# Issuing the clears of a scatter target before two batches' routing instead of behind it

## The chip, the cores and the metric

The kernel runs on one core of a Trainium2 chip. The metric is device microseconds (us) of one execution; the time of a kernel is the median over its runs. The profile is of one execution of its own.

## What is computed

An attention block, then two mixture-of-experts layers with top-1 routing, all in float32.

```python
# attention, per batch (4) and head (8): 512 tokens and 32 states of 64
a  = softmax(x @ state.T / 8);   xread = a @ state
a2 = softmax(state @ x.T / 8);   sread = a2 @ x
x  = concat(xread, sread)  ->  2176 rows of 512

# layer 1 (with a capacity per expert) and layer 2 (without), 8 experts
logits = x @ w_gate
e, gate = argmax(logits), softmax(logits)[argmax]
out[i]  = gate[i] * (relu(x[i] @ w1[e]) @ w2[e])     # w1: 512x1024, w2: 1024x512
# layer 1: a token beyond its expert's capacity gives a row of zeros
```

## The kernel before

**Rows in DRAM.** Attention writes its 2176 rows to `xrows`, 513 words each: 512 values and the gate. The values go out by batch, the gate column later by stores of single words, two per batch (L667, L668, inside `route`). Layer 1 gathers its tokens from `xrows` and scatters its results to `yrows`, of the same shape, from which layer 2 gathers. A token over capacity is never scattered, so `yrows` is first cleared as a whole: `fills` issues four DMAs from a tile of zeros (L711).

**Stages.** An expert's tokens are worked off in quads of 4 x 128 tokens, one quad to a stage. The first stage of a layer is that of the most popular expert, whose first tokens are listed early, before all batches are routed. A stage runs eight columns of `m1_quad` (h = relu(x w1), L1062 to L1065) and `m2_quad` (y += h w2, L1073), interleaved: `(1,0) (1,1) (2,0) (1,2) (2,1) ... (2,7)`. Float32 products are made from hi and lo parts. ScalarE casts the hi part and GpSimd or VectorE subtracts to get the lo part, for weights (`wsplit`, L277 and L278; `split1`, L1291 and L1292) and for tokens and h alike. Beside the quads, experts with few rows left run alone as "small" experts straight from the raw weights (L1221).

**The end of a stage.** `tail` runs the last columns of a stage. Among them it puts the gathers of the next quad's tokens on GpSimd (`gather`, L580), the casts of the next w1's first halves on ScalarE (`split1`, L1291), and the transposes of the gathered tokens on TensorE (`x_quad`, L1032). Each engine works in program order, so a cast that waits for its weights holds the ReLU (L1064) behind it.

**Queues.** Weights, row stores, clears and the zeroing of the output are all issued by SP, in program order, on one DMA queue. Gathers and scatters are GpSimd's own, on another. The next expert's weights (`wload`, L273) can be issued only when the chip has counted the tokens: `planned(0)` copies the counts to `ri` (L1507), and SP reads its branch and the expert's number from there. In the first stage four chunks of w1, four of w2 and eight for a small expert are issued in this order.

**The background list.** What is not TensorE's main work stands in a list of generators, `bgq`, and is woven into the program when it is built. `tick(n)` takes up to n steps of the generator at its head and goes on to the next when that one ends. The first layer's first stage calls `tick(4)` after each part of a column (three parts for `m1_quad`, four for `m2_quad`). A generator that yields `PAUSE` ends the tick; `abreast` takes steps of several in turn and pauses only when all of them do. When the stage begins, the rest of `route(1, 1)` (the second batch's routing) is still at the head. The list then gets the routing of the third and fourth batch (`route(2, 2)`, which ends with their gate stores) abreast of the second batch's list (`enlist_batch(1)`); the clears (`fills`, one step); the plan of the stages (`plan_runs`) abreast of the last two lists; and the reading out of the lists (`plan_lists`).

Of the kernel before, what the change touches and what calls it, by code (L numbers as in the profile page):

```python
# [74 lines left out]
def moe_kernel(ctx: ExitStack, tc: tile.TileContext, x, state, wg1, w1a, w2a, cap, wg2, w1b, w2b, out):  # L75
# [24 lines left out]
    bgq = deque()  # L100
# [14 lines left out]
    def named(name, g):  # L115
        yield from g
        done.add(name)
# [9 lines left out]
    def abreast(*gs):  # L127


        gs = [[g, -1] for g in gs]  # L130
        while gs:
            n = 0
            for s in list(gs):
                if s[1] == clock[0]:
                    continue
                n += 1
                try:
                    if next(s[0]) is PAUSE:
                        s[1] = clock[0]
                    else:  # L140
                        yield
                except StopIteration:
                    gs.remove(s)
            if not n:
                yield PAUSE
# [240 lines left out]
    def list_out(pool, L, g, m, sv, u, w):  # L386

        if g is not None:
            DVE.tensor_scalar(g, sv, -1.0, 0.0, op0=ALU.add, op1=ALU.max)
            yield  # L390
        DVE.tensor_scalar(u, sv, 0.5, FAR, op0=ALU.is_lt, op1=ALU.mult)
        DVE.tensor_scalar(m[:, :, 2], sv, 0.5, None, op0=ALU.is_gt)
        yield
        DVE.scalar_tensor_tensor(out=m[:, :, 3], in0=sv, scalar=-1.0, in1=u, op0=ALU.add, op1=ALU.add)
        yield
        if L == 0:
            DVE.tensor_scalar(w, m[:, :, 3], 1.0 / P, 0.5 / P - 0.5, op0=ALU.mult, op1=ALU.add)
            yield
            DVE.tensor_scalar(m[:, :, 0], w, MAGIC, MAGIC, op0=ALU.add, op1=ALU.subtract)
            yield  # L400
            DVE.scalar_tensor_tensor(out=w, in0=m[:, :, 0], scalar=-float(P), in1=m[:, :, 3], op0=ALU.mult, op1=ALU.add)
            yield
            DVE.tensor_scalar(m[:, :, 1], w, 1.0, None, op0=ALU.add)
            yield
# [141 lines left out]
    def plan_lists(pool, L):  # L546

        mk, no = rt.pop("plan")
        la = pool.tile([KH, 2, P], F32, tag="la", name="la")
        lb = pool.tile([KH, 2, P], F32, tag="lb", name="lb")  # L550
        DVE.tensor_copy(lb, listp[:, :, 1])
        yield
        DVE.scalar_tensor_tensor(out=la, in0=listp[:, :, 0], scalar=float(P), in1=lb, op0=ALU.mult, op1=ALU.add)
        yield PAUSE
        for h in range(2):
            PE.matmul(pyv[:, 0:NT], la[:, h], mk[:, h], start=(h == 0), stop=(h == 1))
        sel = pool.tile([P, NT], F32, tag="sel", name="sel")
        DVE.tensor_copy(sel, pyv[:, 0:NT])
        yield
        DVE.tensor_scalar(rows[L], sel, -1.0, 0.0, op0=ALU.add, op1=ALU.max)  # L560

        ss = sel[:, ML * QT:NT]
        DVE.tensor_scalar(no, no, ss[:, 2 * NA:2 * NA + 1], None, op0=ALU.mult)
        yield
        DVE.tensor_tensor(out=no, in0=no, in1=ss[:, 0:2 * NA].rearrange("p (a b) -> p a b", b=2)[:, :, 0], op=ALU.add)
        yield
        DVE.tensor_scalar(rows1[L], no, -1.0, 0.0, op0=ALU.add, op1=ALU.max)
        u = pool.tile([P, NT], F32, tag="plu", name="plu")
        w = pool.tile([P, NT], F32, tag="plw", name="plw")
        yield from list_out(pool, L, None, md[L], sel, u, w)  # L570
# [6 lines left out]
    rp = ctx.enter_context(tc.tile_pool(name="route", bufs=1))  # L577
# [19 lines left out]
    def pauses(n):  # L597
        for _ in range(n):
            yield PAUSE

    def idle(n):
        for _ in range(n):
            yield
# [23 lines left out]
    def route(b0, nb, then=(), quick=False):  # L627

        n, run = nb * (R + 1), runs_[0]
        lg = lgs[:, b0:b0 + nb].rearrange("p b r e -> p (b r) e")  # L630
        gt = gts[:, b0:b0 + nb].rearrange("p b r -> p (b r)")
        ohb = rtp.tile([P, nb, R + 1, E], BF16, tag="oh", name="oh")
        oh = ohb.rearrange("p b r e -> p (b r) e")
        mv = []
        yield from argmax_onehot(rtp, lg, n, smask[:, 0:nb].rearrange("p b r -> p (b r)"), oh, mv)
        m, v = mv
        cs = rtp.tile([P, nb, R, E], BF16, tag="cs", name="cs")
        rs = rtp.tile([P, nb, 2, E], BF16, tag="rs2", name="rs2")
        DVE.tensor_copy(rs[:, :, 1], ohb[:, :, R])
        DVE.tensor_copy(cs[:, :, 1], ohb[:, :, 0])  # L640
        yield
        for r in range(2, R):
            DVE.tensor_tensor(out=cs[:, :, r], in0=cs[:, :, r - 1], in1=ohb[:, :, r - 1], op=ALU.add)
            yield
        DVE.tensor_tensor(out=rs[:, :, 0], in0=cs[:, :, R - 1], in1=ohb[:, :, R - 1], op=ALU.add)
        yield
        yield from pauses(QUICK[0]) if quick else idle(IDLE[0])
        w = nb * 2 * E
        rsv = rs.rearrange("p b a e -> p (b a e)")
        PE.matmul(pyv[:, 0:w], upper, rsv, start=True, stop=True)  # L650
        PE.matmul(pyv[:, w:2 * w], ones, rsv, start=True, stop=True)
        prs = rtp.tile([P, 2, nb, 2, E], F32, tag="prs", name="prs")
        DVE.tensor_copy(prs.rearrange("p t b a e -> p (t b a e)"), pyv[:, 0:2 * w])
        yield
        preb = rtp.tile([P, nb, R + 1, E], F32, tag="pre", name="pre")
        pre = preb.rearrange("p b r e -> p (b r) e")
        for i in range(nb):
            for a, r in ((0, 0), (1, R)):
                DVE.tensor_tensor(out=preb[:, i, r], in0=run, in1=prs[:, 0, i, a], op=ALU.add)
                DVE.tensor_tensor(out=run, in0=run, in1=prs[:, 1, i, a], op=ALU.add)  # L660
                yield
        yield from then

        def gates():
            yield from gate_of(rtp, lg, m, n, gt)
            for b in range(b0, b0 + nb):
                SP.dma_start(out=xrows[b * ST:b * ST + S, DM:ROW].rearrange("(p r) o -> p r o", p=P), in_=gts[:, b, 0:R, None])  # L667
                SP.dma_start(out=xrows[b * ST + S:(b + 1) * ST, DM:ROW], in_=gts[0:NS, b, R:R + 1])  # L668

        res = []  # L670

        def places():
            DVE.tensor_tensor(out=preb[:, :, 1:R], in0=cs[:, :, 1:R], in1=bc(preb[:, :, 0:1], [P, nb, R - 1, E]), op=ALU.add)
            yield
            far = rtp.tile([P, n, E], F32, tag="far", name="far")
            DVE.tensor_tensor(out=far, in0=pre, in1=bc(cape[:, None, :], [P, n, E]), op=ALU.is_ge)
            yield
            DVE.scalar_tensor_tensor(out=pre, in0=far, scalar=FAR, in1=pre, op0=ALU.mult, op1=ALU.add)
            yield
            yield from slots(rtp, oh, v, pre, n, res)  # L680

        yield from abreast(places(), gates())
        for i in range(nb):
            pp_[b0 + i] = [t[:, i * (R + 1):(i + 1) * (R + 1)] for t in res]
# [3 lines left out]
    def enlist_batch(b, quick=False, eng=(DVE, DVE, POOL)):  # L688

        pp, ek = pp_[b]  # L690
        todo = []
        for r in range(R + 1):
            np_ = P if r < R else NS
            oc = lsp.tile([P, NK], BF16, tag="loc", name="loc")
            ov = lsp.tile([P, 2, P], BF16, tag="lov", name="lov")
            yield from enlist(oc, ov, eng, np_, pp[:, r:r + 1], ek[:, r:r + 1], tida[:, b, r:r + 1], tidb[:, b, r:r + 1], todo)
            if len(todo) > LAG[b]:
                enlist_mm(*todo.pop(0))
        yield from pauses(QUICK[1]) if quick else idle(IDLE[1])
        while todo:  # L700
            enlist_mm(*todo.pop(0))
            yield from () if quick else idle(IDLE[2])
# [3 lines left out]
    def fills(*parts):  # L706

        g = NTOK // P
        for i in parts:
            lo, hi = g * i // 4, g * (i + 1) // 4  # L710
            SP.dma_start(out=yrows.rearrange("(g p) w -> p g w", p=P)[:, lo:hi], in_=bc(zeros[:, None, :], [P, hi - lo, ROW]))  # L711
        yield
# [813 lines left out]
    POOL.memset(meta, 0.0)  # L1526
    POOL.memset(ysb[:, 0], 0.0)
    POOL.memset(ysb[:, NY - 2:NY], 0.0)
    bgq += [abreast(route(2, 2, (), True), enlist_batch(1, True)), fills(0, 1, 2, 3), abreast(plan_runs(rp, 0), named("lists", chain(enlist_batch(2, True), enlist_batch(3, True)))), plan_lists(rp, 0)]
    for t in range(QT):  # L1530
        x_quad(t, ysb[:, 1 + t], py[t], gq[0])
    st = stage(0, 0, [(PLANNED[0], lambda: planned(0)), (READY, room)], TQ)
# [53 lines left out]
```

## Time and profile before

| | |
|---|---|
| median of 3 runs | 507.88 us (507.73 to 507.91) |
| profiled execution, own time | 511.39 us |
| its span, first to last instruction | 509.5 us |
| mean granted TensorE clock | 0.948 |
| TensorE (PE) matmuls, busy | 445.8 us (87%) |
| VectorE (DVE) busy | 195.2 us (38%) |
| ScalarE (ACT) busy | 165.9 us (33%) |
| GpSimd (POOL) busy | 216.5 us (42%) |
| SP's DMA queue: bytes, share of the 16 engines' span | 72.43 MB, 44.5% |
| GpSimd's DMA queue | 15.76 MB, 9.0% |

The shares are means over stages that differ. What holds TensorE in one stage is read from that stretch alone: the waits of TensorE and of the engine in front of it, and the DMA share of the stretch. A clock of 1.00 is 2.4 GHz, 0.50 is 1.2 GHz; a number between is a mean over a stretch that had both.

### The profile page before, as it was taken

What the parts mean: (1) busy time and instruction counts of PE and PEld (TensorE: products, weight loads), DVE (VectorE), ACT (ScalarE), POOL (GpSimd) and SP (SyncE); (2) the same over time, 40 slices, a digit from 0 to 9 for tenths busy, and PEclk for the clock granted to TensorE, in tenths of its full rate; (3) what the DMA queues carried; (4) which work ended last, traced back from release to release, by engine and by line L of the source; (5) the groups of instructions that cost most, each with busy time, mean ns of one, the idle gap of its engine ahead of it and who ended that gap; (6) DMA issues with size and microseconds to landing.
All of it is one profiled execution on the core that took longest, in us unless ns stands there. A gap on an engine that the chain in (4) does not pass through costs nothing. (4 is left out here: it accounts for less than half of the span.)

```text
span 509.5 us, 7964 instructions
## 1 busy us (share of the span) xinstructions
PE 445.8 (87%) x2629; PEld 326.0 (64%) x2629; DVE 195.2 (38%) x666; ACT 165.9 (33%) x288; POOL 216.5 (42%) x197
## 2 busy tenths in 40 slices
PE   8969586979879989999997959999999999999940
PEld 5647365757664775676874748778745847668830
DVE  7967757895040161041264041584410100411110
ACT  4647434210143412345311334312431213451010
POOL 6432742564413445415446403357553506774030
PEclk9999878988979999999999988999999999999995
DMA  8264757079989996909633100025997848200020
GB/s 244 72 151 117 206 135 202 1 175 182 316 305 364 371 381 196 366 24 346 251 132 122 43 11 4 0 95 193 376 388 267 318 171 279 94 28 1 3 93 3
DMA packets 47364, 89.49 MB, mean 176 GB/s; under 512 B 8592, under 2 KB 21136, under 8 KB 47248
## 3 DMA queue, kind: packets, MB, share of 16 engines
q1 hardware_dynamic: 42128, 72.43, 44.5%
q0 software_dynamic: 5120, 15.76, 9.0%
q8 instruction: 43, 0.70, 0.6%
q14 instruction: 73, 0.60, 0.4%
HBM read 67.70 MB, written 21.52 MB: 175 GB/s over the span
## 5 line engine op out<-in xcount | busy, mean ns | idle before, releaser
L1065 DVE SCALAR_TENSOR_TENSOR hTl<-ph,hTh 128x512 fp32r<-128x512 f32 x48 | 33.2, 691 | 206.3 <-ACT hTh L1064 194.8
L1073 PE MATMUL py<-w1h,hTh 128*128 128x512 f32 x192 | 82.6, 430 | 0.0
L1073 PE MATMUL py<-w1l,hTh 128*128 128x512 f32 x192 | 76.4, 398 | 0.0
L1073 PE MATMUL py<-w1h,hTl 128*128 128x512 f32 x192 | 76.4, 398 | 0.0
L278 POOL TENSOR_TENSOR w1l<-raw,w1h 128x1024 fp32r<-128x1024 f32 x22 | 52.6, 2395 | 53.3 <-ACT w1h L277 53.2
L1292 POOL TENSOR_TENSOR w0l<-raw,w0h 128x512 fp32r<-128x512 f32 x40 | 51.0, 1287 | 56.0 <-ACT w0h L1291 51.2
L1064 ACT ACTIVATE hTh<-ph 128x512 fp32r<-128x512 f32 x48 | 28.7, 597 | 127.3 <-PE ph L1062 89.2
L1062 PE MATMUL ph<-xTh,w0h 128*128 128x512 f32 x192 | 54.4, 406 | 7.4 <-issue 5.5
L1062 PE MATMUL ph<-xTl,w0h 128*128 128x512 f32 x192 | 57.2, 421 | 0.0
L1062 PE MATMUL ph<-xTh,w0l 128*128 128x512 f32 x192 | 55.5, 411 | 0.3 <-issue 0.3
L1062 PEld LDWEIGHTS ph<-xTh,w0h 128*128 128x128 f32 x192 | 36.3, 193 | 16.4 <-issue 8.8
L1062 PEld LDWEIGHTS ph<-xTl,w0h 128*128 128x128 f32 x192 | 36.0, 194 | 13.4 <-issue 6.6
L1073 PEld LDWEIGHTS py<-w1h,hTh 128*128 128x128 f32 x192 | 37.1, 193 | 9.5 <-issue 3.4
L1073 PEld LDWEIGHTS py<-w1h,hTl 128*128 128x128 f32 x192 | 36.9, 192 | 8.3
L1073 PEld LDWEIGHTS py<-w1l,hTh 128*128 128x128 f32 x192 | 37.2, 194 | 7.0 <-issue 1.0
L1062 PEld LDWEIGHTS ph<-xTh,w0l 128*128 128x128 f32 x192 | 35.3, 192 | 9.9 <-issue 3.4
L1091 POOL DMA_INDIRECT out_dram<-ysb,dsti x15 | 14.9, 993 | 60.2 <-ACT ysb L1081 52.1
L1291 ACT CAST w0h<-raw 128x512 fp32r<-128x512 f32 x40 | 24.0, 618 | 22.1 <-DMA raw<-in_moe_w_dram 20.8
L1091 POOL DMA_INDIRECT yrows<-ysb,dsti x16 | 15.9, 996 | 29.6 <-DVE oc L336 8.4
L277 ACT CAST w1h<-raw 128x1024 fp32r<-128x1024 f32 x24 | 25.1, 1045 | 5.9 <-issue 5.9
L340 POOL TENSOR_SCALAR lov<-iofb,rpp,tidb 128x128 bf16<-128x128 bf16 (+1 forms) x20 | 16.6, 838 | 15.0 <-DVE rek L330 15.0
L880 PE MATMUL pav<-vg,e1T 128*128 128x264 f32 x56 | 18.0, 450 | 1.2 <-ACT xr L881 1.2
(325 smaller groups left out, 646.5 us busy)
## 6 DMA issues: line engine op xcount, KB each, us to landing
raw<-in_moe_w_dram SPq DMA_DIRECT2D x104, 512.0 KB
out_dram<-zb SPq DMA_DIRECT2D x2, 2176.0 KB
xrows<-xr SPq DMA_DIRECT2D x16, 256.0 KB
yrows<-zeros SPq DMA_DIRECT2D x3, 1026.0 KB
xb<-in_x_dram SPq DMA_DIRECT2D x6, 512.0 KB
yrows<-zeros SPq DMA_DIRECT2D x1, 1282.5 KB
xb<-in_x_dram SPq DMA_DIRECT2D x4, 256.0 KB
st<-in_state_dram SPq DMA_DIRECT2D x1, 256.0 KB
```

The source lines that it names most:

```text
L277: ACT.copy(h, t)
L278: (POOL if on[c] else DVE).tensor_tensor(out=l, in0=t, in1=h.bitcast(F32), op=ALU.subtract)
L340: eng[2].tensor_scalar(ov[0:np_, 1], iofb[0:np_], pp[0:np_], tb[0:np_], op0=ALU.is_equal, op1=ALU.mult)
L880: PE.matmul(pv[:, a, 0:GW], e1_[b][:, r % 2, a, r // 2], vg[:, b, a], start=True, stop=True)
L1062: PE.matmul(p, w[k][:, 0, c * P:(c + 1) * P], u[:, k], start=(i == 0 and k == 0), stop=(i == 2 and k == NC1 - 1))
L1064: ACT.activation(out=hTh[:, c % 2], in_=p, func=AF.Relu)
L1065: DVE.scalar_tensor_tensor(out=hTl[:, c % 2], in0=p, scalar=0.0, in1=hTh[:, c % 2].bitcast(F32), op0=ALU.max, op1=ALU.subtract)
L1073: PE.matmul(py[t], u[:, c % 2, t * P:(t + 1) * P], w[c // 2][:, c % 2], start=(c == 0 and i == 0), stop=(c == NC2 - 1 and i == 2))
L1091: i = POOL.indirect_dma_start(out=(yrows if L == 0 else out)[:, :], out_offset=bass.IndirectOffsetOnAxis(ap=dsti[:, y:y + 1], axis=0), in_ ...
L1291: ACT.copy(h, t)
L1292: (POOL if ON[half][c] else DVE).tensor_tensor(out=l, in0=t, in1=h.bitcast(F32), op=ALU.subtract)
```

## The change

The clears move from the second place of the list to the first. They are then issued by SP in front of the third and fourth batch's gate stores instead of behind them.

```diff
-    bgq += [abreast(route(2, 2, (), True), enlist_batch(1, True)), fills(0, 1, 2, 3), abreast(plan_runs(rp, 0), named("lists", chain(enlist_batch(2, True), enlist_batch(3, True)))), plan_lists(rp, 0)]
+    bgq += [fills(0, 1, 2, 3), abreast(route(2, 2, (), True), enlist_batch(1, True)), abreast(plan_runs(rp, 0), named("lists", chain(enlist_batch(2, True), enlist_batch(3, True)))), plan_lists(rp, 0)]
```

## Rows read from the trace of the kernel before

**Rows 1.** Table of stretches: start:end, length, busy per engine, TensorE clock, DMA share, GB/s.
```profile
90.00:106.00 16.00, 15.78 (x76) 12.60 (x75) 13.49 (x58) 4.87 (x7) 8.17 (x9) 1.00 0.04 1
106.00:116.00 10.00, 6.42 (x26) 4.38 (x25) 9.70 (x50) 0.20 (x1) 6.82 (x8) 0.80 1.04 251
116.00:124.00 8.00, 8.00 (x36) 6.15 (x35) 3.23 (x11) 0.40 (x1) 1.72 (x3) 0.82 1.09 187
...
132.00:144.00 12.00, 7.60 (x37) 5.50 (x36) 1.72 (x3) 4.43 (x8) 5.12 (x4) 0.95 0.91 329
144.00:150.00 6.00, 6.00 (x20) 4.92 (x20) 3.00 (x10) 1.87 (x3) 0.00 (x0) 0.54 0.79 284
```

**Rows 2.** Timeline of SP's DMA queue: start, duration, issuing line.
```profile
86.99 0.61 SPq L668 DMA_DIRECT2D xrows<-gts  x1
102.90 0.52 SPq L667 DMA_DIRECT2D xrows<-gts  x1
...
105.47 3.46 SPq L711 DMA_DIRECT2D yrows<-zeros  x4
115.78 34.19 SPq L273 DMA_DIRECT2D raw<-in_moe_w_dram  x16
```

**Rows 3.** DMA issues of the page: size of one, count.
```profile
yrows<-zeros SPq DMA_DIRECT2D x3, 1026.0 KB
...
yrows<-zeros SPq DMA_DIRECT2D x1, 1282.5 KB
```

**Rows 4.** Timeline of ScalarE, first layer, first and fourth of four casts.
```profile
133.36 0.62 ACT L1291 CAST w0h<-raw 128x512 fp32r<-128x512 f32 x1 [7.99 <-DMA raw<-in_moe_w_dram]
...
141.83 0.62 ACT L1291 CAST w0h<-raw 128x512 fp32r<-128x512 f32 x1 [1.89 <-DMA raw<-in_moe_w_dram]
```

**Rows 5.** Timeline of TensorE, end of the first stage and start of the next.
```profile
135.77 0.39 PE L1073 MATMUL py<-w1h,hTh 128*128 128x512 f32 x1
...
138.05 0.66 PE L1032 MATMUL ph<-ident,xg 128*128 128x128 f32 x4 [1.44 <-DMA xg<-xrows,rows]
...
143.72 1.11 PE L1032 MATMUL ph<-ident,xg 128*128 128x128 f32 x4 [2.85 <-DVE hTl L1065]
...
150.82 1.08 PE L1062 MATMUL ph<-xTh,w0h 128*128 128x512 f32 x4
...
153.20 1.08 PE L1221 MATMUL pyT<-raw,xTf 128*64 128x512 f32 x4
```

**Rows 6.** Timeline of TensorE, the same instructions at a later stage's end.
```profile
217.64 0.39 PE L1073 MATMUL py<-w1h,hTh 128*128 128x512 f32 x1
...
221.73 0.60 PE L1032 MATMUL pyT<-ident,xg 128*128 128x128 f32 x4
...
224.94 1.09 PE L1062 MATMUL ph<-xTh,w0h 128*128 128x512 f32 x4
```

**Rows 7.** Timeline of GpSimd: gathers of the first stage, first, second and last.
```profile
125.05 1.10 POOL L580 DMA_INDIRECT xs<-xrows,rows  x1 [7.33 <-DVE md L392]
126.45 1.00 POOL L580 DMA_INDIRECT xg<-xrows,rows  x1 [0.30 <-issue]
...
130.36 1.00 POOL L580 DMA_INDIRECT xg<-xrows,rows  x1 [0.30 <-issue]
```

**Rows 8.** Timeline of SP's DMA queue in the second layer's first stage.
```profile
348.60 16.73 SPq L273 DMA_DIRECT2D raw<-in_moe_w_dram  x11
```

**Rows 9.** Timeline of ScalarE there: first and fourth cast.
```profile
352.34 0.62 ACT L1291 CAST w0h<-raw 128x512 fp32r<-128x512 f32 x1 [3.50 <-DMA raw<-in_moe_w_dram]
...
358.93 0.62 ACT L1291 CAST w0h<-raw 128x512 fp32r<-128x512 f32 x1 [3.18 <-DMA raw<-in_moe_w_dram]
```

**Rows 10.** Table of stretches, the second layer's first stage.
```profile
348.00:366.00 18.00, 18.00 (x88) 14.87 (x88) 6.32 (x17) 7.29 (x13) 10.15 (x9) 1.00 0.92 335
```

**Rows 11.** Who waited for whom, TensorE, 100 to 130 us: total, times, longest.
```profile
PE listp L346 <- DVE lov L338: 3.6, 3, 1.4
```

**Rows 12.** Instructions on yrows: durations min/median/max, first and last start.
```profile
L1091 POOL DMA_INDIRECT yrows<-ysb,dsti x16: 971/980/1067, 184.3 to 341.7; - x16
```

## The prediction

> **What bounds the kernel now.** I read the profile's page first, then the chain of waits by engine, then the stretch from 86 to 166 us engine by engine, and last two later places where the same code runs without the clears. TensorE sets the pace almost everywhere, so a transfer matters only where TensorE, or an engine that feeds it, stands still for it. The reader is to look for such a place near the clears.
>
> The table of stretches shows it [rows 1]. From 90 to 106 us the DMA engines are nearly empty (share 0.04) while TensorE works 15.78 of 16 us. From 106 us on they are full (share above 1), and what they move is the clears: four issues at 105.47 us [rows 2], 3 x 1026 + 1282.5 = 4360.5 KB or 4.47 MB in all [rows 3]. At the rates of [rows 1], 2.51 MB pass from 106 to 116 us and 1.50 MB from 116 to 124 us, together 4.0 MB, so the clears fill the queue beyond 124 us. The loads of the next expert's weights are issued on the same queue at 115.78 us [rows 2]. ScalarE wants the first of them at 125.4 us (it idles 7.99 us and goes on at 133.36 us) and gets the fourth at 141.83 us [rows 4].
>
> These casts stand in ScalarE's order in front of the ReLU that TensorE needs, and the gathered tokens come late too. TensorE therefore waits 1.44 us for a gather and 2.85 us for the lo part of h, and runs at 0.54 of its clock from 144 to 150 us [rows 1, 5]. The tail of this stage, from the second-to-last column's products to the first product of the next stage, takes 150.82 - 135.77 = 15.05 us [rows 5]. The same instructions in a later stage, with nothing late, take 224.94 - 217.64 = 7.30 us [rows 6]. The difference, 7.75 us, is what late transfers cost here: 4.29 us of waits and some 3.4 us of slow clock (0.46 of 6 us plus 0.05 of 12 us, [rows 1]).
>
> **The change, part by part.** It moves one generator ahead of another in the background list. No transfer or instruction is added or removed.
>
> *The four clears on SP's queue.* They now follow the last gate store of the second batch, which leaves SP at 86.99 + 0.61 = 87.60 us [rows 2]. SP needs 3.46 us to issue them, so it is done near 91.1 us, and its next instruction waits for VectorE's gates until 102.90 us [rows 2]. SP's own time costs nothing, covered by 11.8 us of waiting. The transfers take 4.47 MB at 251 to 187 GB/s [rows 1], that is 17.8 to 23.9 us, and end between 105.4 and 111.5 us, mostly in the stretch that was empty.
>
> *The two batches' gate stores.* They are issued when they were, and stand behind what is left of the clears: they start up to 111.5 - 102.9 = 8.6 us later. The first reader of those rows is the gather at 125.05 us, which waits for VectorE's row numbers [rows 7]. So 13 us cover them and the cost is 0. Were the cover gone, each us would be a us on the gathers.
>
> *The weight loads.* They wait for the counts, not for the clears, and stay at 115.78 us. What they then meet is an empty queue. The trace has that case: in the second layer the same loads are issued at 348.60 us, the first cast runs at 352.34 us and the last at 358.93 us, with the gathers beside them [rows 8, 9], and TensorE works 18.00 of 18.00 us from 348 to 366 us [rows 10]. That is 3.74 and 10.33 us after the issue. Here it gives 119.5 and 126.1 us, before 133.36 and 141.83 us [rows 4]. The ReLU behind the fourth cast is wanted where the tail begins, at 135.77 us [rows 5], so the whole stall goes and the tail should run as in [rows 6]: **-7.75 us**.
>
> *The place in the background list.* A tick of this stage takes four steps and the clears are one. Counting by the code, the steps of the third and fourth batch's routing and of the second batch's list come one step later at first. The routing's four pauses then take up the shift, since a pause ends its tick wherever it falls, and the gates come in the same tick as before. From there the planning starts one step earlier. Where this could be felt is TensorE's wait for list rows, three times and 3.6 us in all, at most 1.4 us [rows 11]. One list product that moves by a part gives or takes at most that; I take 0 and keep +-1.4 us.
>
> *Engines beside the clears.* From 100 to 130 us, with the clears on the wire most of the time, TensorE waits for list rows alone, for no DMA and no fetch [rows 11]. So clears under TensorE's work cost 0. From the other side, if the 3.6 us were the clears' doing, they would move with them and add nothing.
>
> *The readers of yrows.* The first scatter into the cleared rows is at 184.3 us [rows 12], far behind in either order: 0.
>
> Sum: 0 + 0 - 7.75 + 0 + 0 + 0 = -7.75 us. Against the profiled execution that is 511.39 - 7.75 = 503.64 us. The median of the runs shown is 3.51 us below that execution, and I take the saving off it: 507.88 - 7.75 = **500.1 us**.
>
> **Weighed against it.** The gather for the first of the next stage's four groups of tokens is issued at 126.45 us, and TensorE waits for it until 138.05 us, 11.60 us later [rows 5, 7]. The Trainium skill, page "DMA: Bandwidth & Descriptors", section "Queues, rings and completion order", says that a DMA engine takes the queues that have work in turn, packet by packet. By that rule the gathers, on GpSimd's queue, need not wait for the clears to end, and would stay as late as long as any loads run beside them. By the row of the second layer they come in time beside loads (500.1 us); by the rule the sum is that of the first rival.
>
> **The rivals.**
> - *The gathers become what is late.* They are still issued at 126.45 to 130.36 us and share the engines with weight loads. If each again lands 11.60 us after its issue, the last lands at 141.96 us. It is wanted at 135.77 + (221.73 - 217.64) = 139.86 us [rows 5, 6], so TensorE waits 2.1 us, with up to half of the 3.4 us of slow clock behind it: 502.2 to 503.9 us. For it: gathers and loads do overlap. Against: [rows 8 to 10].
> - *The small expert's weights come late.* Eight of the sixteen loads in [rows 2] are for the small expert, read by TensorE at 153.20 us now [rows 5] and at 145.45 us then. Twelve loads of 0.52 MB and five gathers of 128 rows of 2052 bytes, read and written, are 8.9 MB. From 115.78 us at 329 GB/s this ends at 142.9 us, in time, at 284 GB/s at 147.2 us, 1.7 us late [rows 1]: 501.9 us.
> - *The clears are not what the loads wait for.* Then the casts stay and the time is 507.9 us. For it: gathers and loads share the same stretch. Against: the loads take 17.6 us to the first cast here and 3.74 us in the second layer.
> - *Slower: the gate stores, now behind the clears, hold the gathers.* The gathers read rows whose last column these stores write. If the clears in their new place run so slowly that the stores land after the gathers' issue, each us is a us of TensorE at the tail. It turns to a loss beyond 125.05 + 7.75 = 132.8 us, that is, below 4.47 MB / 45 us = 99 GB/s; at 90 GB/s they end at 137.3 us, 12.2 us late, for 512 us. For it: stores of single words behind a full queue are nowhere in the trace. Against: the slowest rate of the clears seen is 187 GB/s [rows 1].
>
> **How the numbers follow.** The full saving: 66%, with its own range of 498.7 to 501.5 us from the +-1.4 us of list waits. The two partial cases: 20%, 501.9 to 503.9 us. No change: 7%. Slower: 7%. The range from 498.7 to 503.5 us holds the first and most of the second, about 80%. Within 0.2% (1.0 us) is what a measurement of this kernel can't tell from no change. Faster by more has 0.86 (both upper cases), the same 0.07, slower 0.07.
>
> **What would show it.** In the profile after, the clears should be issued near 87.6 us and the stretch from 90 to 106 us should be full. ScalarE's casts of the four chunks should run without a wait for DMA, the tail from the second-to-last column to the next stage's first product should take about 7.3 us, and the clock should stay at 1.00 from 144 to 150 us. From there on everything should stand some 7.8 us earlier, to the end. TensorE waiting for gathers at the tail would speak for the first rival, for raw near 145 us for the second, an unchanged wait of the casts for the third, and GpSimd's first gather after 125 us waiting for a store for the last. The prediction is wrong if the earlier tail meets a later wait that gives the time back: the stretches after 150 us would then move by less than the tail did.

## The result and the profile after

In the first set of runs the changed kernel took 499.42 us (median of 4 runs, 498.86 to 500.16) and the kernel before 507.81 us (4 runs, 504.62 to 507.91): a ratio of 0.985, 95% interval 0.981 to 0.989. The forecast was 500.1 us. Two more sets, each on one chip of its own, gave 0.998 (0.994 to 1.002) and 0.990 (0.986 to 0.994). A median here is over all runs of a set, while a ratio and its interval leave out the runs that are more than 1.5% above the fastest run of the same kernel. By these intervals the change is faster in the first and the last set and not to be told from no change in the middle one. How that goes with one mechanism is what the experiments are about.

The table of stretches after, with the columns of [rows 1]:

```profile
90.00:106.00 16.00, 14.60 (x72) 11.25 (x70) 13.88 (x63) 3.34 (x5) 8.48 (x8) 1.00 1.05 199
106.00:116.00 10.00, 8.26 (x25) 5.98 (x26) 7.28 (x41) 0.60 (x1) 4.47 (x7) 0.66 0.48 167
116.00:124.00 8.00, 8.00 (x42) 6.29 (x41) 3.88 (x15) 1.22 (x2) 3.10 (x3) 1.00 1.00 363
132.00:144.00 12.00, 12.00 (x64) 7.95 (x61) 5.13 (x15) 5.26 (x8) 2.36 (x1) 1.00 1.06 385
144.00:150.00 6.00, 6.00 (x30) 2.88 (x28) 0.77 (x2) 2.19 (x4) 1.29 (x1) 1.00 1.09 390
```

The stretch that was empty is full (share 1.05), and the next one is half empty (0.48) before the weight loads come. From 132 to 150 us TensorE works 18.00 of 18.00 us at a clock of 1.00, where it had 13.60 us [rows 1]. The timeline of SP's queue after, to [rows 2]:

```profile
84.42 0.61 SPq L668 DMA_DIRECT2D xrows<-gts  x1
85.12 3.49 SPq L711 DMA_DIRECT2D yrows<-zeros  x4
98.91 0.53 SPq L667 DMA_DIRECT2D xrows<-gts  x1
...
109.99 17.92 SPq L273 DMA_DIRECT2D raw<-in_moe_w_dram  x16
```

The clears stand right behind the second batch's gate stores, and the sixteen loads pass in 17.92 us instead of 34.19 us. The timelines of ScalarE and then of TensorE after, to [rows 4] and [rows 5]:

```profile
122.01 0.62 ACT L1291 CAST w0h<-raw 128x512 fp32r<-128x512 f32 x1 [1.48 <-issue]
...
126.20 1.65 ACT L1291 CAST w0h<-raw 128x512 fp32r<-128x512 f32 x3
```

```profile
130.94 0.39 PE L1073 MATMUL py<-w1h,hTh 128*128 128x512 f32 x1
...
135.02 0.60 PE L1032 MATMUL pyT<-ident,xg 128*128 128x128 f32 x4
...
138.23 1.09 PE L1062 MATMUL ph<-xTh,w0h 128*128 128x512 f32 x4
...
140.62 3.65 PE L1221 MATMUL pyT<-raw,xTf 128*64 128x512 f32 x16
```

No cast waits for a load any more. The four casts are over before the tail begins, at 130.94 us, and the tail takes 138.23 - 130.94 = 7.29 us where 7.30 us was forecast. Nothing in it waits, neither for a gather nor for h.

The span is 11.2 us shorter, more than the tail's 7.76 us. Some 4.0 us of it lie ahead of the place where TensorE forms the third and fourth batch's place sums (L650: 95.55 us before, 91.57 us after). 2.6 us of these stand there before the changed place is reached: the first product of the stage begins at 83.41 us in the one and 80.84 us in the other. The other 1.4 us go with TensorE's clock: from 84 to 100 us it is 0.89 before and 1.00 after, and over all fourteen profiles of this document L650 comes 10.3 to 10.7 us behind that product where the clock there is 1.00 (after, e2, e3, e4) and 11.9 to 13.3 us where it is 0.84 to 0.93 (the ten others). The clears don't decide it: with them on the wire in that stretch it is 1.00 in two profiles (after, e3) and 0.89 to 0.93 in four (e1, e8, e9, e10). So the 4.0 us belong to the two executions and not to the change.

From here on the stretch from L650 (two of the expectations below call it the second batch's place sums) to the end of the second stage is compared; both ends are first or only instructions of their kind, and what runs between is the same work in all kernels. It takes 224.94 - 95.55 = 129.39 us before and 212.30 - 91.57 = 120.73 us after.

### The profile page after: what moved, and what is told of

The parts are those of the page before. It is cut to its first block, busy times and chain, and to the rows that moved or that the text cites. A ratio compares the mean times of both kernels' runs of the same rounds, so it can differ in the third digit from the quotient of the medians.

```text
span 498.3 us, 7961 instructions
## 1 busy us (share of the span) xinstructions
PE 441.2 (89%) x2629; PEld 324.5 (65%) x2629; DVE 197.7 (40%) x666; ACT 166.2 (33%) x288; POOL 217.0 (44%) x197
## 5 line engine op out<-in xcount | busy, mean ns | idle before, releaser
L1292 POOL TENSOR_TENSOR w0l<-raw,w0h 128x512 fp32r<-128x512 f32 x40 | 51.0, 1292 | 50.1 <-ACT w0h L1291 48.3
L1062 PEld LDWEIGHTS ph<-xTl,w0h 128*128 128x128 f32 x192 | 35.9, 194 | 13.2 <-issue 6.6
L880 PE MATMUL pav<-vg,e1T 128*128 128x264 f32 x56 | 17.0, 431 | 1.2 <-ACT xr L881 1.2
```

The lines of the kernel that those rows point to most:

```text
L880: PE.matmul(pv[:, a, 0:GW], e1_[b][:, r % 2, a, r // 2], vg[:, b, a], start=True, stop=True)
L1062: PE.matmul(p, w[k][:, 0, c * P:(c + 1) * P], u[:, k], start=(i == 0 and k == 0), stop=(i == 2 and k == NC1 - 1))
L1292: (POOL if ON[half][c] else DVE).tensor_tensor(out=l, in0=t, in1=h.bitcast(F32), op=ALU.subtract)
```

## The experiments

Each of the sets 2 to 4 was made on one chip, beside the kernel before. The kernel before was not profiled in set 2. The table puts the profiles together. The lag is from the issue of the first weight load to the first cast of w1; the tail and the stretch are as above; the next stage goes from its first product to that of the one behind it. "Free" beside a lag says that the profile puts no idle time of these casts down to a load, or, in e10, no more than the 1.5 us that ScalarE idles there in the changed kernel too. All in us, worked out from the timelines of SP, ScalarE and TensorE.

| profile | clears | lag | tail | next stage | stretch |
|---|---|---|---|---|---|
| before, set 1 | behind | 17.6 | 15.05 | 74.1 | 129.4 |
| e12, before, set 4 | behind | 18.0 | 12.33 | 76.2 | 128.2 |
| e5, before, set 3 | behind | 15.4 | 7.94 | 77.8 | 125.9 |
| e6, before, set 3 | behind | 14.5 | 7.93 | 75.5 | 123.6 |
| e2, step alone, set 2 | behind | 14.6 | 9.37 | 75.4 | 124.5 |
| after, set 1 | in front | 12.0, free | 7.29 | 74.1 | 120.7 |
| e1, after, set 2 | in front | 12.5, free | 7.31 | 74.1 | 121.2 |
| e9, after, set 4 | in front | 12.3, free | 7.31 | 74.1 | 121.0 |
| e3, clears alone, set 2 | in front | 11.9, free | 7.29 | 74.1 | 121.3 |
| e10, half in front, set 4 | half | 12.4, free | 7.30 | 74.1 | 121.1 |
| e11, a quarter more, set 4 | behind | 23.5 | 11.43 | 76.6 | 132.6 |
| e4, behind the loads, set 2 | later | 15.7, free | 11.11 | 81.4 | 132.2 |
| e8, twice, set 3 | in front | 13.2 | 14.37 | 74.1 | 128.2 |
| e7, twice, set 3 | behind | 24.0 | 9.45 | 75.0 | 144.2 |

**e1, e9: the changed kernel again.** No edit.

> The changed kernel once more, beside the kernel before on one chip, for the size of the gain. If the whole gain is the first stage's tail (15.05 us with late transfers, 7.30 us without), it is 7.75 us: about 500 us where the kernel before takes 507.8, a ratio near 0.985. The profile of the changed kernel showed its tail at 7.29 us but a span 11.2 us shorter; if something beside the tail is gained in every execution, the ratio is nearer to 0.978.

> The changed kernel against the one before once more, for the size of the gain: it was 7.6 us in the first comparison and 1 to 2 us in the second, while the stretch from the second batch's place sums to the end of the second stage was shorter by 2.5 to 8.3 us in every pair of profiles. If the stall before is a matter of how late the loads land in that execution, the tail of the changed kernel is 7.3 us again and the ratio lies between 0.984 and 0.998. If the first comparison's 7.6 us were the true size, the ratio is 0.983 to 0.987.

Measured in set 2: 499.21 us (12 runs, 495.87 to 501.96) against 501.29 us (29 runs, 496.36 to 507.95), ratio 0.998 (0.994 to 1.002). In set 4: 506.21 us (12 runs, 501.01 to 513.68) against 512.12 us (24 runs, 506.64 to 519.20), ratio 0.990 (0.986 to 0.994). The tail is 7.31 us in both profiles, so it does not differ from set to set in the changed kernel. The whole gain of 7.75 us that e1 was to show did not show. The profiled run of e9 is among the longest of its twelve (511.95 us); its extra time lies behind the stretch, in the third stage, which takes 76.7 us where it takes 66.9 us in e1.

**e2, e3: the two halves of the change.** The background list is moved by one step without the clears, and the clears without the step.

```diff
 # e2 (the clears take no step)
-    bgq += [fills(0, 1, 2, 3), abreast(route(2, 2, (), True), enlist_batch(1, True)), ...
+    bgq += [idle(1), abreast(route(2, 2, (), True), enlist_batch(1, True)), fills(0, 1, 2, 3), ...
 # e3 (the clears take no step)
-    bgq += [fills(0, 1, 2, 3), abreast(route(2, 2, (), True), enlist_batch(1, True)), ...
+    bgq += [fills(0, 1, 2, 3), abreast(route(2, 2, (), True), enlist_batch(1, True)), idle(1), ...
```

> The clears stay behind the two batches' routing and gate stores, but without a step of the background list; an empty step stands in front of the routing instead. So the routing, the lists and the plan are woven in as in the changed kernel, and only the place of the clears is the old one. If the clears' place makes the gain: within 0.3 us of the kernel before (507.8 us), clears issued after the gate stores near 105 us, tail near 15 us. If the moved steps of the background list make it: near 500 us.

> The other half: the clears are issued in front of the routing, but without a step; an empty step stands where they were. The instructions of the other engines keep their old weaving. If the clears' place makes the gain: near 500 us, tail near 7.3 us, within 1.4 us of the changed kernel. If the moved steps make it: near 507.8 us.

Measured: e2 502.29 us, ratio 1.005 (1.001 to 1.008); e3 501.69 us, ratio 0.998 (0.993 to 1.003), both against 501.29 us. The first cast, the tail's first product and the next stage's first product, in e2 and then in e3:

```profile
126.24 0.62 ACT L1291 CAST w0h<-raw 128x512 fp32r<-128x512 f32 x1 [5.64 <-DMA raw<-in_moe_w_dram]
...
130.98 0.39 PE L1073 MATMUL py<-w1h,hTh 128*128 128x512 f32 x1
...
140.35 1.09 PE L1062 MATMUL ph<-xTh,w0h 128*128 128x512 f32 x4
```

```profile
124.84 0.62 ACT L1291 CAST w0h<-raw 128x512 fp32r<-128x512 f32 x1 [1.49 <-issue]
...
133.75 0.39 PE L1073 MATMUL py<-w1h,hTh 128*128 128x512 f32 x1
...
141.04 1.09 PE L1062 MATMUL ph<-xTh,w0h 128*128 128x512 f32 x4
```

So e3 has the changed kernel's tail and stretch (7.29 and 121.3 us), and e2 has neither: its tail of 9.37 us and its stretch of 124.5 us lie among those of the kernel before. The clears' place alone removes the stall, and the step by itself does not. The medians do not show it: e3's is as long as that of the kernel before, and 2.5 us above e1's, where at most 1.4 us was expected. Its runs go from 496.15 to 505.34 us, and its profile spends 2.6 us more than e2's ahead of L650 (93.84 against 91.27 us). That difference is there before any clear is issued: the first product of the stage begins at 83.50 us in e3 and 80.54 us in e2. Nor is it known why e2 comes out just above the kernel before. That the tail of e2 is not near 15 us was the first sign that the first profile of the kernel before was not typical.

**e5, e6, e12: the kernel before, three more profiles.** No edit.

> The kernel before itself, one profile more, since its times on the second chip (496 to 508 us) show that its executions differ. If the late loads cost the same 7.75 us in every execution, the tail is near 15 us again and the first cast stands some 17.6 us behind the issue of the loads. If they cost what the execution's own pace makes of them, the tail lies anywhere between 7.3 and 15 us, with the casts 14 to 18 us behind the issue, and the clock falls behind the tail's waits only where they are long.

> The same once more, for the spread between two profiles of one kernel on one chip: the same tail within 0.3 us if it is fixed, another one if it is not. The first stage from its first product to the second batch's place sums is run by both kernels alike, and differed by 2.6 us in the profiles of the changed kernel; if that is the clock, the stretch from 70 to 100 us shows it.

> A third look at the kernel before on this chip, for the tail and the small expert's stage: the four casts 14 to 18 us behind the issue of the loads, the tail between 7.8 and 15 us, the next stage 0 to 4 us longer than the 74.1 us of the changed kernel.

Measured: 507.54, 502.98 and 510.47 us, one run each, with tails of 7.94, 7.93 and 12.33 us. (e5's run is longer than each of the seven others of the kernel before in set 3, 498.02 to 503.13 us.) e6 was to show whether the clock makes the difference ahead of L650: from the stage's first product on the difference goes with it, as said above, but not up to there, since the clock from 70 to 84 us is 0.74 in e6 and 0.99 in e12, and the product begins at 81.97 us in the one and at 83.65 us in the other. ScalarE's casts in e6 and e12, first and last of each:

```profile
129.46 0.62 ACT L1291 CAST w0h<-raw 128x512 fp32r<-128x512 f32 x1 [4.92 <-DMA raw<-in_moe_w_dram]
...
136.51 0.62 ACT L1291 CAST w0h<-raw 128x512 fp32r<-128x512 f32 x1 [2.06 <-DMA raw<-in_moe_w_dram]
```

```profile
133.63 0.62 ACT L1291 CAST w0h<-raw 128x512 fp32r<-128x512 f32 x1 [8.72 <-DMA raw<-in_moe_w_dram]
...
141.20 0.62 ACT L1291 CAST w0h<-raw 128x512 fp32r<-128x512 f32 x1 [1.88 <-DMA raw<-in_moe_w_dram]
```

The loads were issued at 114.93 and 115.65 us, so the lag is 14.5 us in e6 and 18.0 us in e12. The stretches in which the clears move say part of why, e6 and then e12:

```profile
106.00:116.00 10.00, 6.52 (x24) 4.41 (x24) 9.26 (x51) 0.60 (x1) 7.02 (x10) 0.76 1.06 275
116.00:124.00 8.00, 8.00 (x38) 6.15 (x37) 3.47 (x17) 0.06 (x1) 0.79 (x1) 0.87 1.10 205
124.00:132.00 8.00, 8.00 (x37) 6.50 (x36) 2.79 (x9) 2.28 (x4) 6.54 (x7) 1.00 1.02 310
132.00:144.00 12.00, 11.67 (x60) 9.24 (x59) 5.11 (x15) 5.25 (x9) 3.69 (x3) 1.00 0.93 336
```

```profile
106.00:116.00 10.00, 6.62 (x26) 4.41 (x25) 9.73 (x50) 0.17 (x1) 6.82 (x8) 0.75 1.03 251
116.00:124.00 8.00, 8.00 (x38) 6.20 (x37) 3.63 (x14) 0.43 (x1) 1.75 (x3) 0.89 1.09 198
124.00:132.00 8.00, 8.00 (x37) 6.52 (x36) 2.44 (x10) 0.60 (x1) 5.11 (x5) 1.00 1.03 208
132.00:144.00 12.00, 7.74 (x39) 5.67 (x38) 2.34 (x5) 4.64 (x9) 5.13 (x4) 1.00 0.97 333
144.00:150.00 6.00, 6.00 (x30) 4.48 (x29) 3.47 (x12) 3.17 (x6) 0.00 (x0) 1.00 0.87 304
```

The queue moves 275 and 205 GB/s in e6 and 251 and 198 GB/s in e12, and from 124 to 132 us e6 moves 310 GB/s, e12 still 208. The trace also has every DMA packet with its size, and a row of the clears is one of 2052 bytes. By these the 4.47 MB take 20.1 us in e6 (105.59 to 125.68 us) and 21.8 us in e12 (106.40 to 128.17 us), and they end 10.8 us behind the issue of the loads in the one and 12.5 us in the other. So the slower clears are 1.8 us of the 3.5 us by which the lags differ. The other 1.7 us lie between the last packet of the clears and the first cast, where the loads share the engines with the gathers (first packets at 128.5 and 129.9 us). No run shows what of these 1.7 us is the gathers' doing. With these lags TensorE's waits in its tail are 0.33 us in all in e6 and 4.2 us in e12:

```profile
137.45 0.66 PE L1032 MATMUL ph<-ident,xg 128*128 128x128 f32 x4 [1.32 <-DMA xg<-xrows,rows]
...
143.10 0.66 PE L1032 MATMUL ph<-ident,xg 128*128 128x128 f32 x4 [2.85 <-DVE hTl L1065]
```

The tails go in the order of the fourth cast, whose ReLU the prediction had as wanted where the tail begins. It starts 1.55 us behind the tail's first product in e5 and e6, 2.96 us in e2, 5.91 us in e12 and 6.06 us in the first profile; in the changed kernel it is over before.

Where the tail gets off lightly the next stage pays. TensorE in e5, the small expert's products (L1221) in the next stage:

```profile
145.93 2.27 PE L1221 MATMUL pyT<-raw,xTf 128*64 128x512 f32 x8 [0.43 <-DMA raw<-in_moe_w_dram]
...
148.40 1.08 PE L1221 MATMUL pyT<-raw,xTf 128*64 128x512 f32 x4 [0.20 <-DMA raw<-in_moe_w_dram]
...
149.70 1.08 PE L1221 MATMUL pyT<-raw,xTf 128*64 128x512 f32 x4 [0.22 <-DMA raw<-in_moe_w_dram]
```

The same sixteen products run without a gap in the changed kernel (140.62 us, above). In e6 the two groups of the small expert take 4.19 and 4.29 us to the next product, against 3.58 us each in the changed kernel: 1.3 us of that stage's 1.4 us. In e5 the stage takes 3.8 us more, and its clock is 0.72 from 166 to 172 us.

**e10, e11: less and more behind the gate stores.**

```diff
 # e10, on the changed kernel: two clears in front (one step), two behind (no step)
+    bgq += [fills(0, 1), abreast(route(2, 2, (), True), enlist_batch(1, True)), fills(2, 3, step=False), ...
 # e11, on the kernel before: the first clear once more, behind the four
+    bgq += [abreast(route(2, 2, (), True), enlist_batch(1, True)), fills(0, 1, 2, 3, 0), ...
```

> Two of the four clears in front of the routing, two behind its gate stores (without a step). The two behind (2.36 MB, about 11 us) are through near 112 to 116 us, when the weight loads are issued. If the loads' queue is what costs, the casts wait little or nothing, the tail is near 7.3 us and the time is that of the changed kernel. If anything of the clears behind the gate stores costs, half of the difference to the kernel before is left.

> The kernel before with a fifth clear of 1.05 MB behind its four, some 4.5 to 5 us more in front of the weight loads. If the kernel before stands at the edge of its cover, where each us by which the loads land later is a us at the tail or more, with the clock falling once the waits are long, the tail grows from about 8 us to 12 to 16 us, as long as in the first profile of the kernel before, and the time by 4 to 9 us against the kernel before on this chip. If the stall is proportional to the clears, it grows by a quarter of 3 to 5 us, about 1 us.

Measured: e10 508.19 us, ratio 0.995 (0.991 to 0.999); e11 514.77 us, ratio 1.012 (1.007 to 1.018). In the profile e10 has no stall at all (tail 7.30 us, stretch 121.1 us). Its first cast (L1292 in this kernel):

```profile
128.44 0.62 ACT L1292 CAST w0h<-raw 128x512 fp32r<-128x512 f32 x1 [1.49 <-DMA raw<-in_moe_w_dram]
```

It runs 12.4 us behind the issue of the loads and only 2.1 us behind the ReLU ahead of it, as in the changed kernel, where ScalarE idles 1.48 us in this place with no load late. In the profiles without a stall ScalarE comes to this cast 11.9 to 12.5 us behind the issue, so a load that lands by then costs nothing, and the 14.5 us of e6 already go with a stretch that is 2.5 us longer. The times are less clear: e10's median lies between those of e9 (506.21 us) and of the kernel before (512.12 us); a third of the difference is left by the medians, half of it by the ratios. With e9's runs spread over 12.7 us and e10's over 8.2 us, the medians don't settle whether e10 has the whole gain. In e11 the first cast comes 23.5 us behind the issue, 5.6 us later than in e12, and the stretch is 4.4 us longer. Its tail is not the 12 to 16 us expected but 11.43 us. The rest of the stall has moved ahead of the tail, where TensorE waits for the ReLU behind the first cast:

```profile
PE py L1073 <- ACT hTh L1064: 4.2, 1, 4.2
```

The proportional rival, about 1 us, falls: the lower end of the interval is 0.7%, some 3.5 us.

**e7, e8: the clears twice.**

```diff
 # e7, on the kernel before
+    bgq += [abreast(route(2, 2, (), True), enlist_batch(1, True)), fills(0, 1, 2, 3, 0, 1, 2, 3), ...
 # e8, on the changed kernel
+    bgq += [fills(0, 1, 2, 3, 0, 1, 2, 3), abreast(route(2, 2, (), True), enlist_batch(1, True)), ...
```

> The kernel before with its clears issued twice, behind the routing: 8.9 MB in front of the weight loads instead of 4.47 MB. If the loads wait for the clears, the four casts move back by the second set's 19 to 22 us and, with the stall already begun, the tail grows by nearly all of that: 515 to 530 us. If the loads are late for another reason (the gathers, their own rate), the time stays within 3 us of the kernel before.

> The changed kernel with its clears issued twice, in front of the routing: some 40 us of clears from 86 us on, to 125 us or a little beyond. The loads issued near 111 us then stand behind them again, and the gate stores do too. If the empty stretch is what hides the clears, it is overfull now and the time goes back to that of the kernel before or some us more: 500 to 512 us, with casts waiting for raw 14 to 20 us behind the issue. If the gate stores behind the clears hold the gathers (the rival on the slower side), GpSimd's first gather waits for a store of the gates until the clears are through, and TensorE waits for the gathered rows at the tail; its wait is then as long as the gathers are late.

Measured against 500.56 us (7 runs): e7 520.24 us, ratio 1.037 (1.031 to 1.043); e8 508.31 us, ratio 1.014 (1.008 to 1.020). Both sets clear the same rows, so SP issues the second only as the first lands; it waits 18.3 us in e8, and the loads themselves go out later (131.14 us in e7, 119.86 us in e8). In e7 the tail is only 9.45 us, for the stall lies ahead of it: TensorE waits 19.5 us for the ReLU behind the first cast. The pair shows that the cover has an end: with 8.9 MB in front the stall is back. It shows the slower rival too. GpSimd's first gather in e8, and then what TensorE waits for at the tail:

```profile
132.24 1.10 POOL L580 DMA_INDIRECT xs<-xrows,rows  x1 [15.93 <-issue]
133.66 1.00 POOL L580 DMA_INDIRECT xg<-xrows,rows  x1 [0.32 <-issue]
```

```profile
PE ph L1032 <- DMA xg<-xrows,rows: 4.2, 1, 4.2
```

The gather starts at 132.24 us; in e5 and e6, on that chip, ScalarE's ReLU behind the same row numbers and the gather are within 0.3 us of each other, and that ReLU runs at 123.57 us in e8. It is some 8.5 us late, and what it still needs are the rows whose gates stand behind the clears. SP itself issues these stores late, from 109.51 to 118.85 us. By the packets, their single words of 4 bytes pass from 123.0 to 129.5 us, beside the last of the clears (to 128.2 us), and the gather starts 2.7 us after them. The order in time fits; that the gather waits for these stores is still argued and not shown, since the trace names no releaser.

**e4: the clears behind the eight weight loads.**

```diff
+    bgq += [idle(1), abreast(route(2, 2, (), True), enlist_batch(1, True)), abreast(plan_runs(rp, 0), ...
 ...
         for i in range(2):
             load_next(L, 1, i)
+        if L == 0:
+            run_all(fills(0, 1, 2, 3))
```

> The clears are issued behind the eight loads of the next expert's weights, in front of the small expert's eight; an empty step stands in front of the routing. If what counts is that the weight loads don't stand behind the clears: the four casts wait no more than in the changed kernel and the tail is near 7.3 us. But the clears (some 20 us) then stand in front of the small expert's weights, which TensorE reads about 10 us after the tail begins, so a wait of TensorE for raw of 5 to 12 us should appear there and the time lie between 503 and 510 us. If it counts that the clears use the empty stretch at 90 to 106 us, in which nothing else is on the wire, and not which loads they delay, the tail keeps a part of its stall. If instead the clears disturb TensorE's neighbours wherever they run, the clock or the list waits change where they now run, and not at the small expert.

Measured: 510.14 us, ratio 1.021 (1.015 to 1.027). No cast waits for a load, as expected (the first idles 5.21 us for nothing that the profile shows, and TensorE does not wait for it), but the tail is 11.11 us and not near 7.3 us. TensorE's waits from 128 to 166 us:

```profile
PE pyT L1221 <- DMA raw<-in_moe_w_dram: 4.6, 1, 4.6
PE ph L1032 <- DMA xg<-xrows,rows: 2.0, 1, 2.0
```

The gathers now run beside the clears, and TensorE waits 2.0 us for the first: issued at 123.77 us, used at 135.15 us. The small expert's weights come behind the clears and cost 4.6 us; the clock is 0.86 from 132 to 144 us and 0.81 from 150 to 165 us. It is not enough that the weight loads overtake the clears. The clears have to be through before the loads, the gathers and the small expert's weights want the queues.

## Why the prediction was right, and where it was off

*The clears' place.* Right: issued 0.1 us behind the second batch's gate stores, and moved in the stretch that was empty. Their last packet ends at 105.55 us, 20.4 us behind the issue, inside the 17.8 to 23.9 us taken. SP's 3.49 us were covered.

*The gate stores.* Right at this size: their words are on the wire from 103.0 us, 4.1 us behind the first issue where it was 1.2 us before, and through at 106.1 us. GpSimd's first gather runs at 120.22 us after a wait for VectorE, not for a store. The cover that was named is real. e8 overfills the stretch, and the gather and TensorE behind it are late.

*The weight loads and the tail.* The mechanism is right in each profile. In all four with the clears in front, once (after, e1, e3, e9), no cast waits for a load and the tail is 7.29 to 7.31 us; e2 and e3 give it to the clears' place alone. **The term that was mis-sized is the -7.75 us.** It was the difference of two tails in one execution and was taken for the kernel. In the five profiles with the clears behind, once (before, e2, e5, e6, e12), the stretch is 2.5 to 8.3 us longer than the mean of those four (121.1 us), 5.2 us in the mean. The execution that the prediction used had nearly the longest lag (17.6 us), and it alone among them lost 3 us and more to the slow clock in the tail: e12, with the same two waits of TensorE (2.85 us for h and 1.32 us for the gather), keeps a clock of 1.00 from 132 to 150 us and has a tail of 12.33 us instead of 15.05 us. That the median came out 0.7 us from the forecast is luck. In that set three of four runs of the kernel before lay at 507.7 to 507.9 us, and the two medians differ by 8.4 us; in set 2 they differ by 2.1 us and in set 4 by 5.9 us. The stretches go the same way, by one profile of each kernel: 8.7 us in set 1, 3.3 us in set 2 (where e2 has to stand for the kernel before) and 7.2 us in set 4.

*Where the rest of the stall lies.* The prediction put all of it into the tail and the small expert's weights among the rivals of the changed kernel. In e2, e5, e6 and e12 a part of it (1.3 to 3.8 us) lies in the next stage of the kernel before, where the small expert's weights come late. In the changed kernel that stage takes 74.1 us every time, as it does in the profile that the prediction used.

*The moved step.* Right: 0. e3's tail and stretch are the changed kernel's with the old weaving, and TensorE's waits for list rows are 2.7 us in all after, 3.6 us before [rows 11].

*The gathers.* TensorE takes the first group at 131.62 us, 10.0 us behind its issue, without a wait; the first rival fell. In e4 the gathers end while the clears are still on the wire: TensorE has the first group at 135.15 us, and SP waits for the clears until 146.73 us. The Trainium skill, page "DMA: Bandwidth & Descriptors", section "Queues, rings and completion order", has a DMA engine take its queues in turn; e4 agrees, at 11.4 us for a gather beside the clears.

*What stays open.* Whatever the kernel, L650 comes at 91.27 to 97.67 us, and what is left behind the second stage takes 282.2 to 286.0 us, in e9 293.2 us; the sets differ by more (medians of the kernel before of 500.6 to 512.1 us). The clock from 84 to 100 us is a part of it; for the rest no run here tells why, nor why the clears take 20.1 us on one chip and 21.8 us on another, nor why e3's median does not show the gain that its profile shows. The prediction took 1.0 us as what a measurement can't tell from no change; with runs of one kernel spread over up to 13 us in a set, the intervals here reach some 2 us to either side or more.

## What to carry to other kernels

A bulk transfer that nothing waits for belongs in a stretch where its queue is empty, early enough to be through before anything urgent is issued behind it. Merely letting the most urgent loads overtake it moves the stall to the next reader. Before the length of a stall is taken as the gain, measure it in several executions. This stall sits at the edge of its cover, between 12.5 and 14.5 us of lag: from e6 to e12 the clears end 1.8 us later and the stretch is 4.6 us longer, and the clock adds its own part only in some executions.

## What the runs showed of the hardware

The clears, 4.47 MB in rows of 2052 bytes from one tile of zeros, took 19.1 to 22.3 us from first to last packet where they were issued once and in one piece, 200 to 233 GB/s. The DMA engines' share was above 1.0 with them (1.05 at 199 GB/s from 90 to 106 us after), where the stretches with the weight loads reach 363 to 390 GB/s at a share of 1.00 to 1.09. A full share of the DMA engines thus says little of the bytes moved. Two waits of TensorE of nearly the same length (1.44 and 2.85 us before, 1.32 and 2.85 us in e12) were followed by a clock of 0.54 from 144 to 150 us in the one execution and of 1.00 in the other.
